# Pair sums and weight blocks placed by a scheduling pass, and operands made from PSUM, in an attention and two-expert kernel

## The chip, the cores and the metric

The kernel runs on one core of a Trainium2 chip. The metric is the device time of one execution in microseconds (us), the median of several runs. The profile shows one execution; its span runs from the first to the last instruction.

## The reference

Attention with pooled queries feeds two dense layers with their own activations. Batch 2, 8 heads, 1152 keys, head size 64; two neighbouring queries are averaged, so that 576 are left for each batch and 1152 tokens in all.

```python
q_pool = q.reshape(B, H, S // 2, 2, D).mean(axis=3)
scores = matmul(q_pool, k.T) / sqrt(D)
attn = exp(scores - max(scores)) / (sum(...) + 1e-9)
x = (attn @ v).transpose(0, 2, 1, 3).reshape(1152, 512)
h = x @ w_in1;  x = maximum(0.01 * h, h) @ w_out1       # 512 -> 2048 -> 512
h = x @ w_in2;  x = (h * tanh(softplus(h))) @ w_out2
```

The weights arrive as 64-bit floats.

## The kernel before

**Precision.** Each fp32 operand of a matmul is split into a rounded high part (a ScalarE cast) and a low part (source minus high part, by GpSimd or VectorE); each product is three matmuls, high by high, high by low and low by high.

**Attention.** Eight pairs of heads (four for each batch), nine tiles of 128 rows for each pair, 72 tiles `n`. A tile has scores (steps A, B, S on TensorE, three PSUM regions of 1152 columns), the maximum (M over 896 columns, N over 256, K for both, VectorE), the exponential (X, ScalarE, with row sums), nine transposes (T), and the split of the transposed tile (H on ScalarE, L on VectorE). P and Q take steps of the products with V and of the next pair's preparation. Scores of even tiles lie in PSUM columns 128 to 1280, those of odd ones in 1280 to 2432; a bank has 512 columns, so bank 2 holds the last 256 columns of even tiles and the first 256 of odd ones. Transposes and results use the columns from 2560.

**Pair sums.** The first layer multiplies 2x2 blocks by Strassen's method in Winograd's form (seven products in place of eight). Its right operands B11, T1, B22, T2, T3, B21 and T4 are blocks of the attention result and their differences. `pair_end_ops` scales a pair's result; `parts_of` then queues two steps (pairs 0 and 1 of a batch) or five (pairs 2 and 3), each a split and often a subtraction that the next step needs. Step V of the order takes one from the queue (`pop_part`). The sums of a pair overwrite those of the pair two before, and a buffer returns after four pairs. `last_recip` and `last_end` do the last pair after all tiles.

**Experts.** Two layers of eight slices of 256 hidden columns. `convert(i)` loads a slice's four blocks of 512 KB, turns each from 64-bit to 32-bit floats (two ScalarE activations, two VectorE bit operations, one GpSimd addition), makes the sums S1, S2, S4, S3 of the weights and splits all. `block_steps(i, g)` has the seven products of six matmuls for batch `g`, with the activation, split again by `finish`; `out_steps` multiplies by `w_out` and adds to `Y` in SBUF. `between(g)` makes layer 2's operands from `Y`.

**Order.** A `Recorder` takes every call as an operation with its memory cells and costs by a table. Up to tile 63 (CUT) all are issued as the hand-written PATTERN has them. The rest are list-scheduled: for each engine the earliest ready operation, ties by due time. An operation made by `lighter` may go to GpSimd or VectorE, whichever comes first; in the fixed order it is GpSimd. Each engine works through its own queue in that order. As all operations are replayed by the recorder, every row of the profile has line L391, and rows are told apart by tile: R holds split operands, F fp32 sums, I raw inputs and integers, PS is PSUM, `in_w_dram` the weights.

Of the kernel before, what the change touches and what calls it, by code (L numbers as in the profile page):

```python
# [19 lines left out]
SQ = S // 2  # L20
# [21 lines left out]
CUT = 63  # L42


class Op:
    __slots__ = ("alts", "reads", "writes", "preds", "succs", "due", "n", "unit", "eng", "end", "go")


class Recorder:
# [5 lines left out]
    def __init__(self, nc, file):  # L55
        self.nc, self.file, self.ops, self.open, self.cut = nc, file, [], None, None
        for name in self.ENGINES:
            setattr(self, name, Proxy(self, name))
# [12 lines left out]
    @contextmanager  # L71
    def either(self):

        assert self.open is None
        self.open = []
        yield
        made, self.open = self.open, None
        self.add([m[:4] for m in made], made[0][4], made[0][5])

    def add(self, alts, reads, writes):  # L80
        op = Op()
        op.alts, op.reads, op.writes, op.preds, op.succs = alts, reads, writes, set(), []
        op.n, op.eng, op.due = len(self.ops), None, 0.0
        self.ops.append(op)
# [22 lines left out]
    def cost(eng, method, outs, ins, kw):  # L107
# [29 lines left out]
    def cells(self, x):  # L137
# [10 lines left out]
        step = 512 if tag == "PS" else 32  # L148
# [15 lines left out]
    def plan(self):  # L164
# [22 lines left out]
        for op in reversed(self.ops):  # L187
            eng, _, occ, fin = op.alts[0]
            if eng != "PE":
                op.due += 3000  # L190
            for s in op.succs:
                lag = (occ if eng == "PE" and s.alts[0][0] == "PE" else fin + self.SYNC)
                op.due = min(op.due, s.due - lag)
# [15 lines left out]

        for op in self.ops[:self.cut]:  # L210
            place(op, op.alts[0])
        rest = self.ops[self.cut:]
        left = {op: sum(p.eng is None for p in op.preds) for op in rest}
        waiting = {op for op in rest if not left[op]}
        while waiting:
            best = {}
            for op in waiting:
                for alt in op.alts:
                    eng = alt[0]
                    t = max(free[eng], ready(op, eng))  # L220
                    key = (t if t > free[eng] + 5 else free[eng], op.due, op.n)
                    if eng not in best or key < best[eng][0]:
                        best[eng] = (key, op, alt)
            key, op, alt = min(best.values(), key=lambda b: b[0][0])
            place(op, alt)
# [7 lines left out]
        tail = sorted(order[self.cut:], key=lambda x: x[0].go)  # L233
        return order[:self.cut] + tail

    def emit(self):
        for op, calls in self.plan():
            for name, method, args, kw, line in calls:
                code = compile("\n" * (line - 1) + "method(*args, **kw)", self.file, "exec")
                exec(code, {"method": getattr(getattr(self.nc, name), method), "args": args, "kw": kw})  # L240
# [11 lines left out]
def tile_attention_moe_moe(  # L252
# [15 lines left out]
    F = sb.tile([128, 10832], F32, name="F")  # L268
# [3 lines left out]
    X = R[:, 0:XW].rearrange("p (g o s k t) -> p g o s k t", g=2, o=7, s=2, k=2)  # L272
    B11, B21, B22, T1, T2, T3, T4 = range(7)
# [26 lines left out]
    rlast = qsum  # L300
# [4 lines left out]
    ebuf = [F[:, 4832 + i * S:4832 + (i + 1) * S] for i in range(3)]  # L305
# [8 lines left out]
    traw = F[:, 4832:4832 + 2304].rearrange("p (o k t) -> p o k t", o=4, k=2)  # L314
    wraw = [I[:, 1024 * i:1024 * i + 1024] for i in range(2)]
    wa = [F[:, 8288 + 512 * i:8800 + 512 * i] for i in range(4)]
    wsum = I[:, 2048:2816].bitcast(F32).rearrange("p (o k f) -> p o k f", o=3, k=2)
    signs = PS[:, 3584:4096].bitcast(I32)
# [310 lines left out]
    def last_recip():  # L629
        after(("I", NPR - 1), mark=("R", 0))  # L630
        for first, c0, n in ((True, 0, 256), (False, 256, 320)):
            bank, col = t_take()
            for t in ((0, 1) if first else (2, 3)):
                c = col + 128 * (t % 2)
                nc.tensor.transpose(PS[:, c:c + 128], rwide[:, 128 * t:128 * t + 128], ident)
            if not first:
                nc.tensor.transpose(PS[:, col + 256:col + 384], rwide[:, 512:640], ident)
            nc.scalar.copy(out=rlast[:, c0:c0 + n], in_=PS[:, col:col + n])
            t_free.append(bank)

    def lighter(**kw):

        with rec.either():
            nc.gpsimd.tensor_tensor(**kw)
            nc.vector.tensor_tensor(**kw)

    def parts_of(p):
# [6 lines left out]
        def minus(to, a, b):  # L654
            lighter(out=to, in0=a, in1=b, op=ALU.subtract)

        def split(o, src):
            hi, lo = (X[:, g, o, i, k] for i in range(2))
            nc.scalar.copy(out=hi, in_=src)
            minus(lo, src, rounded(hi))  # L660

        if j < 2:
            return [
                [lambda: split(B11, q1), lambda: minus(q1, q2, q1)],
                [lambda: split(T1, q1)],
# [4 lines left out]
            [lambda: split(B22, q2), lambda: minus(t1, q2, t1)],  # L670
            [lambda: split(T2, t1), lambda: minus(b12, q2, b12)],
            [lambda: split(T3, b12)],
            [lambda: split(B21, q1), lambda: minus(q1, q1, t1)],
            [lambda: split(T4, q1)],
        ]

    def last_end():
        x = xu[(NPR - 1) % 4]
        after(("R", 0), *(("U", NPR - 1, u) for u in range(4)), *(("E", NPR - 2, i) for i in (True, False)))
        for h in (slice(TH, SQ), slice(0, TH)):  # L680
            lighter(out=x[:, h], in0=x[:, h], in1=rlast[:, h], op=ALU.mult)
            for step in parts_of(NPR - 1)[:3] if h.start else parts_of(NPR - 1)[3:]:
                for f in step:
                    f()
# [23 lines left out]
    banks = [0, 1, 2, 3, 4, 5, 6]  # L708

    def convert(i):  # L710
# [3 lines left out]
        l, s = divmod(i, NSL)  # L714
        w = (w1, w2)[l]
        wi, wo = WI[i % 2], WO[i % 3]

        def block(b):
            a = wa[b]
            ai = a.bitcast(I32)  # L720
            if not wide:
                nc.sync.dma_start(out=a, in_=w[s, b])
                return
            raw = wraw[(4 * i + b) % 2]
            v = raw.rearrange("p (n t) -> p n t", t=2)
            nc.sync.dma_start(out=raw, in_=w[s, b].bitcast(I32))
            nc.scalar.activation(out=a, in_=v[:, :, 1].bitcast(F32), func=AF.Copy, scale=2.0 ** -112)
            nc.scalar.activation(out=v[:, :, 0], in_=v[:, :, 0].bitcast(U32), func=AF.Copy, scale=2.0 ** -29)
            sign = v[:, :, 1] if i < 2 else signs
            nc.vector.tensor_scalar(out=sign, in0=v[:, :, 1], scalar1=-2 ** 31, scalar2=None, op0=ALU.bitwise_and)  # L730
            nc.vector.scalar_tensor_tensor(out=ai, in0=ai, scalar=3, in1=sign, op0=ALU.logical_shift_left,
# [337 lines left out]
```

## Time and profile before

| | |
|---|---|
| median of 3 runs | 705.27 us (704.4 to 707.95) |
| profiled execution: time, span | 707.48 us, 705.6 us |
| mean granted TensorE clock | 0.976 |
| busy: TensorE, its weight loads | 653.4 us (93%), 596.8 us |
| busy: VectorE, ScalarE, GpSimd | 539.3 us, 486.8 us, 459.0 us |
| TensorE waits for ScalarE's F, VectorE's R | 17.4 us (17 times), 14.9 us (17) |
| TensorE waits for ScalarE's R, VectorE's F | 7.4 us (8), 7.1 us (6) |

The attention ends near 300 us, the first layer near 510 us. PE is TensorE, DVE VectorE, ACT ScalarE, POOL GpSimd, SP SyncE.

### The profile page before, as it was taken

What the parts mean: (1) busy time and instruction counts of PE and PEld (TensorE: products, weight loads), DVE (VectorE), ACT (ScalarE), POOL (GpSimd) and SP (SyncE); (2) the same over time, 40 slices, a digit from 0 to 9 for tenths busy, and PEclk for the clock granted to TensorE, in tenths of its full rate; (3) what the DMA queues carried; (4) which work ended last, traced back from release to release, by engine and by line L of the source; (5) the groups of instructions that cost most, each with busy time, mean ns of one, the idle gap of its engine ahead of it and who ended that gap; (6) DMA issues with size and microseconds to landing.
All of it is one profiled execution on the core that took longest, in us unless ns stands there. A gap on an engine that the chain in (4) does not pass through costs nothing.

```text
span 705.6 us, 11839 instructions
## 1 busy us (share of the span) xinstructions
PE 653.4 (93%) x4154; PEld 596.8 (85%) x4154; DVE 539.3 (76%) x1033; ACT 486.8 (69%) x1039; POOL 459.0 (65%) x415
## 2 busy tenths in 40 slices
PE   7899999988979998739999999999899999999997
PEld 5799898977878987639989999999788888998896
DVE  4789897967768989997777778767988676775454
ACT  6789888877868888666766675757486666564330
POOL 6857577685766746986787665766787876574000
PEclk9999999998999999969999999999899999999999
DMA  4323232323212222313332223122112332310003
GB/s 130 117 77 113 82 94 92 80 75 77 80 42 80 47 68 79 116 61 99 110 121 90 91 91 120 60 78 102 31 61 91 119 100 81 121 60 0 1 1 134
DMA packets 18171, 57.77 MB, mean 82 GB/s; under 512 B 2368, under 2 KB 4928, under 8 KB 18112
## 3 DMA queue, kind: packets, MB, share of 16 engines
q1 hardware_dynamic: 16768, 52.18, 22.6%
q0 software_dynamic: 1120, 4.59, 2.8%
q8 instruction: 32, 0.52, 0.3%
q10 hardware_dynamic: 224, 0.26, 0.1%
q14 instruction: 27, 0.22, 0.1%
HBM read 47.71 MB, written 2.36 MB: 71 GB/s over the span
## 4 chain that ended last, share of the span: by engine, by line
PE 65%; POOL 9%; DVE 8%; ACT 6%; DMA 6%; issue 5%; SPq 0%; POOLq 0%; ACTq 0%; DVEq 0%
PE PS L391 65%; POOL R L391 4%; POOL F L391 4%; DVE R L391 4%; ACT F L391 3%; DVE F L391 3%; DMA I<-in_w_dram 3%; ACT R L391 3%; DMA F<-F 3%; DMA I<-in_kT_dram 1%; DVE I L391 0%; DVE PS L391 0%; POOL I L391 0%; ACT I L391 0%; ACT PS L391 0%
## 5 line engine op out<-in xcount | busy, mean ns | idle before, releaser
L391 PE MATMUL PS<-R 128*128 128x288 f32 (+4 forms) x3466 | 599.6, 328 | 42.0 <-ACT F L391 14.3
L391 PEld LDWEIGHTS PS<-R 128*128 128x128 f32 x3466 | 520.1, 192 | 86.6 <-ACT F L391 16.5
L391 DVE TENSOR_TENSOR R<-PS,R 128x384 fp32r<-128x384 f32 (+1 forms) x312 | 156.5, 520 | 54.9 <-ACT R L391 27.5
L391 POOL TENSOR_TENSOR R<-F,R 128x512 fp32r<-128x512 f32 (+4 forms) x116 | 141.3, 1233 | 56.3 <-ACT F L391 42.1
L391 DVE TENSOR_TENSOR F<-PS,F 128x512 f32<-128x512 f32 (+3 forms) x198 | 110.6, 562 | 58.8 <-PE PS L391 58.0
L391 POOL TENSOR_TENSOR F<-F,I 128x512 int32<-128x512 int32 x64 | 86.1, 1348 | 67.9 <-DVE F L391 29.3
L391 DVE TENSOR_REDUCE F<-PS 128x1 f32<-128x256 f32 (+1 forms) x144 | 106.7, 751 | 17.2 <-ACT F L391 9.2
L391 POOL TENSOR_TENSOR R<-I,R 128x576 fp32r<-128x576 f32 (+2 forms) x47 | 93.2, 1984 | 31.0 <-ACT R L391 19.4
L391 ACT CAST R<-PS 128x384 fp32r<-128x384 f32 x216 | 96.8, 485 | 21.7 <-PE PS L391 21.0
L391 PE MATMUL PS<-F 128*128 128x128 f32 x688 | 105.0, 280 | 6.6 <-ACT F L391 3.1
L391 POOL TENSOR_TENSOR F<-F 64x320 f32<-64x320 f32 (+6 forms) x80 | 67.3, 845 | 53.6 <-ACT R L391 24.3
L391 PEld LDWEIGHTS PS<-F 128*128 128x128 f32 x688 | 83.6, 143 | 18.3 <-DVE R L391 6.2
L391 ACT ACTIVATE F<-PS,F 128x1152 f32<-128x1152 f32 x72 | 88.5, 1230 | 3.5 <-PE PS L391 1.7
L391 ACT CAST R<-F 128x512 fp32r<-128x512 f32 (+5 forms) x114 | 62.7, 567 | 35.5 <-POOL F L391 20.5
L391 ACT ACTIVATE R<-PS 128x288 fp32r<-128x288 f32 x96 | 38.8, 407 | 59.3 <-DVE PS L391 55.9
L391 ACT COPY F<-PS 128x288 f32<-128x288 f32 (+2 forms) x130 | 50.7, 399 | 25.9 <-PE PS L391 20.6
L391 ACT ACTIVATE F<-I 128x512 f32<-128x512 f32 x64 | 43.3, 677 | 35.9 <-DMA I<-in_w_dram 28.9
L391 ACT CAST R<-I 128x576 fp32r<-128x576 f32 (+4 forms) x49 | 43.0, 877 | 8.2 <-PE PS L391 6.6
L391 DVE TENSOR_TENSOR R<-F,R 128x288 fp32r<-128x288 f32 (+2 forms) x44 | 41.4, 953 | 7.2 <-ACT F L391 6.1
L391 ACT ACTIVATE I<-I 128x512 int32<-128x512 uint32 x64 | 42.9, 675 | 0.0
L391 DVE TENSOR_SCALAR PS<-I 128x512 int32<-128x512 int32 x56 | 38.5, 687 | 1.5 <-DMA I<-in_w_dram 0.9
L391 ACT ACTIVATE PS<-PS 128x288 f32<-128x288 f32 x96 | 38.7, 404 | 0.0
(28 smaller groups left out, 250.9 us busy)
## 6 DMA issues: line engine op xcount, KB each, us to landing
I<-in_w_dram SPq DMA_DIRECT2D x64, 512.0 KB, 3.3
I<-in_vN_dram SPq DMA_DIRECT2D x8, 576.0 KB, 4.0
R<-R POOLq DMA_DIRECT2D x14, 320.0 KB, 4.2
I<-in_qT_dram SPq DMA_DIRECT2D x7, 576.0 KB, 4.6
I<-in_kT_dram SPq DMA_DIRECT2D x7, 576.0 KB, 4.1
out_dram<-F SPq DMA_DIRECT2D x8, 256.0 KB, 2.0
F<-F SPq DMA_DIRECT2D x16, 80.0 KB, 2.0
F<-F SPq DMA_DIRECT2D x16, 64.0 KB, 1.9
```

Source lines behind the costliest of these rows:

```text
L391: eng.dma_start(out=dst.bitcast(F32), in_=src)
```

## The change

Steps V of the attention and three weight blocks of slice 0 (`stage`, at tiles 12, 27 and 42) are recorded as loose. In the fixed part of the order the planner puts a loose operation ahead of the next one of its engine when, by its table, it would be ready for 300 ns and end no more than 150 ns after that one's start; an operation that needs one not yet placed forces it in. What is left at the cut joins the list schedule, which now has due times that count each engine's queue and may pick a more urgent operation that starts a little later. The last pair's operands and those between the layers are made by VectorE from values kept in PSUM. `lighter` is gone: subtractions are GpSimd's unless VectorE is named. The blocks around both changes of stage are issued in another order, with five PSUM banks instead of seven until the first slice is through, and the converted weight blocks have two buffers, `wa[i % 2]`. Operand X is laid out anew (half `k` outside), and the recorder tells PSUM apart by 128 columns instead of 512.

```diff
+SLIP = 150
+LOOK = 0.6
+STAGE = (12, 27, 42)
...
-            return (n + 62) / 0.96 * (1.4 if both else 1), (n + 145) / 0.96 * (1.4 if both else 1)
+            return (n + 62) / 0.96 * (3 if both else 1), (n + 145) / 0.96 * (3 if both else 1)
...
-        step = 512 if tag == "PS" else 32
+        step = 128 if tag == "PS" else 32
...
+        while heap:
+            op = heapq.heappop(heap)[2]
+            eng, _, occ, _ = op.alts[0]
+            op.due = min(op.due, back[eng] - occ)
+            if eng != "PE":
+                back[eng] = op.due
...
         for op in self.ops[:self.cut]:
+            if op.loose:
+                loose.append(op)
+                continue
+            for p in sorted(op.preds, key=lambda p: p.n):
+                if p.eng is None:
+                    force(p)
+            eng = op.alts[0][0]
+            start = max(free[eng], ready(op, eng))
+            found = True
+            while found:
+                found = False
+                for l in loose:
+                    if l.eng is None and l.alts[0][0] == eng and all(p.eng for p in l.preds):
+                        if max(free[eng], ready(l, eng) + 300) + l.alts[0][2] <= start + SLIP:
+                            place(l, l.alts[0])
+                            found = True
+                            break
             place(op, op.alts[0])
...
+                near = [x for x in ops if x[0] <= t0 + 5]
+                pick = min(near, key=lambda x: x[1:3])
+                soon = [x for x in ops if x[0] <= t0 + LOOK * pick[3].alts[0][2] and x[1] < pick[1] - 1000]
+                if soon:
+                    pick = min(soon, key=lambda x: x[1:3])
...
+    xraw = F[:, 9696:10720].bitcast(I32)
+    strips = bass.AP(tensor=PS.tensor, offset=PS.offset, ap=[list(PS.ap[0]), [2432, 2], [1, 128]]).bitcast(I32)
...
+    def last_pair():
+        low, high, third = (PS[:, c:c + TH] for c in (3072, 2592, 3584))
...
+        nc.vector.tensor_tensor(out=high, in0=high, in1=x[:, TH:SQ], op=ALU.mult)
+        minus(third, high, old[:, 0:TH], nc.vector)
+        part(T2, third)
+        part(B22, high)
+        minus(high, high, old[:, TH:SQ], nc.vector)
+        part(T3, high)
+        nc.vector.tensor_tensor(out=x[:, 0:TH], in0=low, in1=x[:, 0:TH], op=ALU.mult)
+        part(B21, x[:, 0:TH], nc.gpsimd)
+        minus(third, x[:, 0:TH], third, nc.vector)
+        part(T4, third)
...
-    banks = [0, 1, 2, 3, 4, 5, 6]
+    banks = [0, 1, 2, 3, 4]
+    def stage(i, b):
...
+        for c in range(2 if i < 2 else 1):
+            if i < 2:
+                to, top, sign = (y[:, 256 * c:256 * c + 256].rearrange("p (h n) -> p h n", h=2)
+                                 for y in (ai, v[:, :, 1], v[:, :, 1]))
+                sign = strips
+            else:
+                to, top, sign = ai, v[:, :, 1], signs
...
+        def final(d, half, keep):
...
+            y = Y[:, NTOK * d + t0:NTOK * d + t0 + TH]
+            nc.vector.tensor_tensor(out=ps if keep else y, in0=ps, in1=y, op=ALU.add)
...
+            def two():
+                ps = state["b11"][0]
+                state["b12"] = final(k, 1, False)
+                minus(ps, state["b12"], ps, nc.vector)
+                part(T1, ps, nc.vector)
...
-        for f in block_steps(0, 0):
-            f()
-        merged(block_steps(0, 1), out_steps(0, 0))
+        merged(block_steps(0, 0), [])
+        merged(out_steps(0, 0), [])
+        merged(block_steps(0, 1, late=True), [])
+        banks.extend((5, 6))
...
+            if i == NSL - 2:
+                merged(block_steps(i, 0) + block_steps(i + 1, 0), out_steps(i - 1, None))
+                merged(block_steps(i, 1), out_steps(i, 0))
+                convert(i + 2)
+                merged(between(0), block_steps(i + 1, 1))
+                merged(out_steps(i, 1), [])
+            elif i == NSL:
+                first = out_steps(i, None)
+                merged(between(1), block_steps(i, 0, late=True) + first[:4])
+                merged(block_steps(i + 1, 0, late=True), [])
+                merged(block_steps(i, 1, late=True), [])
+                convert(i + 2)
+                merged(block_steps(i + 1, 1, late=True), first[4:])
...
             if xq:
-                for f in xq.pop(0):
-                    f()
+                with rec.loose():
+                    for f in xq.pop(0):
+                        f()
...
+            if n in STAGE:
+                with rec.loose():
+                    stage(0, STAGE.index(n))
...
-        last_recip()
-        last_end()
+        last_pair()
```

## Rows read from the trace of the kernel before

**Rows 1.** The page: busy time of each engine, its share of the span, instructions.
```profile
PE 653.4 (93%) x4154; PEld 596.8 (85%) x4154; DVE 539.3 (76%) x1033; ACT 486.8 (69%) x1039; POOL 459.0 (65%) x415
```

**Rows 2.** By stretch: length, busy PE, PEld, DVE, ACT, POOL, clock, DMA share, GB/s.
```profile
280.00:320.00 40.00, 23.74 (x143) 21.07 (x143) 38.51 (x53) 26.29 (x61) 33.17 (x29) 0.83 0.25 83
285.00:300.00 15.00, 9.99 (x75) 9.02 (x74) 14.97 (x21) 10.62 (x26) 13.30 (x14) 1.00 0.28 89
...
500.00:512.00 12.00, 8.59 (x45) 8.12 (x44) 11.35 (x15) 4.31 (x9) 9.40 (x7) 0.72 0.14 44
516.00:548.00 32.00, 29.18 (x173) 25.52 (x172) 26.25 (x48) 24.17 (x57) 24.83 (x23) 1.00 0.26 83
400.00:490.00 90.00, 90.00 (x597) 86.33 (x596) 67.28 (x132) 57.15 (x131) 56.33 (x49) 1.00 0.28 94
```

**Rows 3.** The same columns, from one kT load to the next.
```profile
39.42:69.67 30.25, 30.08 (x217) 28.14 (x216) 27.72 (x60) 27.22 (x54) 20.54 (x18) 1.00 0.31 91
69.67:102.08 32.41, 31.07 (x220) 28.43 (x218) 28.14 (x61) 27.73 (x56) 22.87 (x21) 1.00 0.31 85
...
134.48:173.24 38.76, 33.52 (x220) 30.55 (x218) 28.87 (x61) 28.81 (x59) 26.72 (x26) 0.91 0.25 71
173.24:211.05 37.81, 32.50 (x220) 29.82 (x219) 28.65 (x61) 28.69 (x59) 26.73 (x26) 0.95 0.25 74
```

**Rows 4.** Timelines of ScalarE and TensorE: start, time, what, wait before it.
```profile
80.37 0.43 ACT L391 CAST R<-F 128x288 fp32r<-128x288 f32 x1 [1.74 <-POOL F L391]
...
159.42 0.43 ACT L391 CAST R<-F 128x288 fp32r<-128x288 f32 x1 [3.46 <-POOL F L391]
...
161.49 0.79 PE L391 MATMUL PS<-R 128*128 128x256 f32 x2 [3.97 <-ACT F L391]
```

**Rows 5.** Groups by shape, whole run: count, busy us, mean ns, waits before.
```profile
L391 POOL TENSOR_TENSOR F<-F,I 128x512 int32<-128x512 int32 x64 | 86.1, 1348 | 67.9 <-DVE F L391 29.3 <-ACT F L391 13.0 <-issue 10.8
...
L391 ACT ACTIVATE F<-I 128x512 f32<-128x512 f32 x64 | 43.3, 677 | 35.9 <-DMA I<-in_w_dram 28.9 <-POOL R L391 4.3 <-POOL I L391 2.6
...
L391 ACT CAST R<-F 128x288 fp32r<-128x288 f32 x28 | 11.8, 435 | 22.3 <-POOL F L391 17.3 <-DVE F L391 5.0
...
L391 DVE COPY F<-PS 128x256 f32<-128x256 f32 x8 | 3.4, 424 | 2.0 <-PE PS L391 2.0
```

**Rows 6.** A bank shared: an exponential in ScalarE's timeline, and VectorE's maxima as a group.
```profile
99.14 1.23 ACT L391 ACTIVATE F<-PS,F 128x1152 f32<-128x1152 f32 x1
...
L391 DVE TENSOR_REDUCE F<-PS 128x1 f32<-128x256 f32 x72 | 30.1, 420 | 15.0 <-ACT F L391 9.2 <-PE PS L391 3.4 <-ACT R L391 1.3
```

**Rows 7.** VectorE's groups by shape, 282 to 320 us.
```profile
L391 DVE TENSOR_TENSOR R<-F,R 128x288 fp32r<-128x288 f32 x9 | 11.7, 1331 | 0.0
L391 DVE TENSOR_TENSOR F<-F 128x288 f32<-128x288 f32 x7 | 9.3, 1341 | 0.2 <-ACT F L391 0.2
...
L391 DVE TENSOR_TENSOR PS<-PS,F 128x288 f32<-128x288 f32 x3 | 1.4, 451 | 0.0
```

**Rows 8.** Timelines of four engines, 290 to 316 us.
```profile
298.20 0.37 ACT L391 COPY F<-PS 128x256 f32<-128x256 f32 x1
...
300.64 1.89 POOL L391 TENSOR_TENSOR F<-F 64x256 f32<-64x256 f32 x2 [0.41 <-DMA F<-F]
...
309.27 6.43 DVE L391 TENSOR_TENSOR R<-F,R 128x288 fp32r<-128x288 f32 x4
...
291.86 2.59 PE L391 MATMUL PS<-R 128*128 128x288 f32 x19
...
311.41 2.82 PE L391 MATMUL PS<-R 128*128 128x288 f32 x10 [5.54 <-DVE R L391]
```

**Rows 9.** VectorE's group from 498 to 516 us, TensorE's wait, the table loads.
```profile
L391 DVE TENSOR_TENSOR R<-F,R 128x576 fp32r<-128x576 f32 x7 | 11.2, 1618 | 0.7 <-ACT R L391 0.7
...
505.45 1.65 PE L391 MATMUL PS<-R 128*128 128x256 f32 x6 [3.20 <-DVE F L391]
...
L391 ACT ACT_TABLE_LOAD x2 | 2.6, 1283 | 1.4 <-PEq L1057 1.4
```

More of the change, by code (lines that the diff above doesn't have):

```diff
@@ L42 @@
 CUT = 63
+SLIP = 150
+LOOK = 0.6
+STAGE = (12, 27, 42)
 class Op:
-    __slots__ = ("alts", "reads", "writes", "preds", "succs", "due", "n", "unit", "eng", "end", "go")
+    __slots__ = ("alts", "reads", "writes", "preds", "succs", "due", "n", "loose", "eng", "end", "go")
 class Recorder:
@@ L71, in either, with loose @@
     @contextmanager
[L72 to L75 removed]
+    def loose(self):
+        self.free = True
         yield
[L77 to L78 removed]
+        self.free = False
     def add(self, alts, reads, writes):
@@ L627, in invert_sums, with minus, split @@
                                 in1=one[0:64].unsqueeze(1).to_broadcast([64, 2, 64]), op=ALU.mult)
[L629 to L645, printed above, removed]
+    def minus(to, a, b, eng=None):
+        (eng or nc.gpsimd).tensor_tensor(out=to, in0=a, in1=b, op=ALU.subtract)
+    def split(pair, src, eng=None):
+        hi, lo = pair
+        nc.scalar.copy(out=hi, in_=src)
+        minus(lo, src, rounded(hi), eng)
     def parts_of(p):
@@ L652, in parts_of, with part @@
         q1, q2 = x[:, 0:TH], x[:, TH:SQ]
[L654 to L660, printed above, removed]
+        def part(o, src):
+            split([X[:, g, k, o, i] for i in range(2)], src)
         if j < 2:
             return [
-                [lambda: split(B11, q1), lambda: minus(q1, q2, q1)],
-                [lambda: split(T1, q1)],
+                [lambda: part(B11, q1), lambda: minus(q1, q2, q1)],
+                [lambda: part(T1, q1)],
             ]
@@ L755, in convert, with block_steps @@
         for f in range(2):
-            block(2 + f)
-            split([wo[:, h, f] for h in range(2)], wa[2 + f])
+            stage(i, 2 + f)
+            split([wo[:, h, f] for h in range(2)], a[2 + f])
     nblock = [0]
-    def block_steps(i, g):
+    def block_steps(i, g, late=False):
         l = i // NSL
@@ L795, in finish @@
             if name is None:
[L796 removed]
+                minus(gl, src, rounded(gh))
             else:
@@ new lines, in between @@
+        wo, gs = WO[i % 3], G[i % 2]
+        def final(d, half, keep):
+            t0 = SQ * g + TH * half
+            b = banks.pop(0)
+            ps = PS[:, 512 * b:512 * b + TH]
+            with rec.unit():
+                for f in range(2):
+                    for j, (ws, gi) in enumerate(PARTS):
+                        nc.tensor.matmul(out=ps, lhsT=wo[:, ws, f, 128 * d:128 * d + 128],
+                                         rhs=gs[f][:, gi, t0:t0 + TH], start=f == j == 0, stop=f == 1 and j == 2)
+            y = Y[:, NTOK * d + t0:NTOK * d + t0 + TH]
+            nc.vector.tensor_tensor(out=ps if keep else y, in0=ps, in1=y, op=ALU.add)
+            if keep:
+                return ps, b
+            banks.append(b)
+            return y
@@ new lines, in rows, with part, one_, three @@
+        def rows(k):
+            state = {}
+            def part(o, src, eng=None):
+                split([X[:, g, k, o, h] for h in range(2)], src, eng)
+            def one_():
+                state["b11"] = final(k, 0, True)
+                part(B11, state["b11"][0], nc.vector)
+            def two():
[3 more added lines that the diff above has]
+                part(T1, ps, nc.vector)
+            def three():
+                ps = state["b11"][0]
+                b22 = final(k + 2, 1, False)
+                minus(ps, b22, ps, nc.vector)
+                part(T2, ps, nc.vector)
+                part(B22, b22)
+                minus(state["b12"], b22, state["b12"])
+                part(T3, state["b12"])
+            def four():
+                ps, b = state["b11"]
+                b21 = final(k + 2, 0, False)
+                part(B21, b21)
+                minus(ps, b21, ps, nc.vector)
+                part(T4, ps, nc.vector)
+                banks.append(b)
+            return [one_, two, three, four]
@@ L909, in merged @@
+        return [f for two in zip(rows(0), rows(1)) for f in two]
     def merged(a, b):
```

198 lines of the change are left out of this document (97 added, 101 removed).

## Prediction

> **What bounds the kernel now.** I read the page first: its busy shares and the slices of the granted clock. TensorE is busy for 653.4 us [rows 1] of the span of 705.6, so what can be won lies in the 52 us in which it stands idle and in the stretches that follow, where it runs at the lower clock. Next I read the busy time by stretch, to see where those are. In the expert layers, away from their two ends, TensorE is busy for all of 90.00 us at clock 1.00 [rows 2]: nothing is to be had there, and nothing may be lost. The holes are in three places.
>
> The first is the attention. Cut at the starts of the kT loads, a pair of heads takes 30.25 us undisturbed, then 32.41, and two pairs take 38.76 and 37.81, though TensorE has 220 matmuls in each of the last three and is busy with them for 31.07 us in the plain one [rows 3]. ScalarE's timeline says why. A cast of a 128x288 pair sum stands in its queue until GpSimd has made that sum: 1.74 us at 80.37 us, the first of six such short waits (also near 113, 145, 184, 222 and 254), and 3.46 us at 159.42, the first of two long ones (the other is at 198.13). Behind the cast wait the casts and the exponential of the running tile, so VectorE and TensorE stop as well; TensorE comes back at 161.49 after 3.97 us [rows 4], and the clock of those pairs falls to a mean of 0.91 and 0.95 [rows 3]. These are the V steps of the hand-written order (pop_part).
>
> The second is the change from attention to experts: from 280 to 320 us TensorE is busy for 23.74 of 40, at clock 0.83, while VectorE is busy for 38.51 [rows 2]. The third is the change between the layers: 8.59 of 12 us from 500, at clock 0.72, and 29.18 of 32 from 516 [rows 2].
>
> **The change, part by part.** *Pair sums.* The pass takes each V step out of the fixed order and puts an instruction on its engine only where the planner sees room. Per disturbed pair the loss is its length less 31.07: 1.34 for one with a short wait, 7.7 and 6.7 for the two with a short and a long one [rows 3]. With the four short waits outside those two, 4 x 1.34 = 5.4, the attention has 19.8 us to give. Moved on GpSimd's queue, the sums pass the next pair's preparation, its two DMA issues and the additions of results; one put in too early holds these up by its own length. GpSimd has the time: it is busy for 26.7 us even in the long pairs, under the 31.07 that TensorE needs. ScalarE and VectorE have less room, 28.8 and 28.9 us of work there [rows 3]. The deadline stays (the sums of two pairs earlier are overwritten), and what has not been placed by then is forced in, waits and all. I take it that both long waits go, (7.7 - 1.34) + (6.7 - 1.34) = 11.7, and half of the six short ones, 4.0: gain 15.7, bounds 0 and 19.8.
>
> *Three weight blocks.* Each is one 512 KB load on SyncE's queue, two 128x512 activations of 0.677 us on ScalarE, four VectorE operations on 128x256 with their sign in two PSUM strips (nearest row: a 128x256 copy out of PSUM, 0.424), and one GpSimd addition of 1.348 [rows 5]. For three blocks that is 4.1, 12 x 0.424 = 5.1 and 4.0 us. The copies of attention results stand behind the loads on SyncE's queue, but a load waits only for its buffer, free since the block 15 tiles before. GpSimd and ScalarE hide their parts in idle time that the rows show; VectorE is the tightest. A second cost is that the strips lie in PSUM banks 0 and 4, which every tile's scores use. The rows show what sharing a bank does: the 128x256 maximum of a tile lies in bank 2 and needs TensorE's scores alone, yet these 72 maxima stood 9.2 us for ScalarE's F, 0.13 each; what writes F there is the exponential, 1.23 us long, which reads the neighbouring tile's columns of that bank [rows 6]. A strip operation can so cost from 0 to 0.424 + 1.23. I take half of VectorE's 5.1, since it is near its limit, and 12 x 0.13 = 1.5 of waits: 4.0; bounds 0 and 12 x 1.65 = 19.8.
>
> [...]
>
> *Attention to experts.* Idle there is 40 - 23.74 = 16.3; the lower clock is 40 x 0.17 = 6.8, of which the busy share, 23.74 / 40, counts: 4.0. So 20.3 us can be had [rows 2]. Today the last pair's products are SBUF work: VectorE's subtractions on 128x288 with both inputs in SBUF took 1.331 us (9) and 1.341 (7), while those with an input in PSUM took 0.451 [rows 7]. After the last attention result leaves PSUM at 298.20 come its copy, GpSimd's addition (from 300.64, 0.95 each of two) and then this work, whose last four take until 315.70; TensorE waits 5.54 us for it [rows 8]. In the new order nine operations of 0.45 are left, 4.1 us, with GpSimd's lone split and ScalarE's casts of 0.435 [rows 5] beside them: 301.6 + 4.1 = 305.7 at the latest, ten us sooner. Meanwhile the outputs of the first block (48 matmuls) and two products that don't need the last pair (12) now stand ahead: 60 x 0.136 (19 took 2.59 [rows 8]) = 8.2 us from 298, to 306. Three blocks less to convert also takes 3 x 1.35 us from GpSimd and VectorE's work on 128x512 from this stretch. What stays is VectorE's latency over the last tiles, 285 to 300, where TensorE idles for 15 - 9.99 = 5.0 us [rows 2], and I leave 1 more: gain 20.3 - 6.0 = 14.3, bounds 4 and 20.3. The two banks withheld at first cost nothing: a block holds three at once.
>
> *Between the layers.* Idle 3.4 and the clock 12 x 0.28 x 8.59/12 = 2.4, then 2.8 more idle: 8.6 to be had [rows 2]. Today VectorE makes the operands with seven 128x576 subtractions of 1.618 us, and TensorE waits 3.20 [rows 9]. The change makes each from PSUM in halves, at 0.451 [rows 7], while TensorE has other blocks' 42 products and 48 output matmuls, 12.2 us. I take all of the first stretch, 5.8, and half of the second: 7.2, bounds 0 and 8.6.
>
> *At nothing.* The subtraction of the slices' c22 moves to GpSimd for good, two a slice and each under the 1.348 us of a 128x512 operation [rows 5], so at most 2.7; GpSimd has 33.7 of 90 us free there [rows 2]. If that cover went, a slice would end up to 2.7 us later. The wider weight buffers and the planner's new due times I put at nothing because TensorE has no idle time to win in the slices, though they can lose some (below).
>
> Sum: 15.7 - 4.0 + 14.3 + 7.2 = 33.2. The profiled execution took 707.48, so 674.3; it lay 2.2 over the median of the runs shown, 705.27, so **672** by that median.
>
> **Rivals.**
> - *The pass finds no room.* VectorE and ScalarE are nearly full in the disturbed pairs, and waits forced at the deadline are the old ones; the blocks still cost 4.0. For it: ScalarE's and VectorE's busy time. Against: GpSimd, whose lateness makes the waits, has 4 us free. Gain 14.3 + 7.2 - 4.0 = 17.5: 688.
> - *The strips serialise the tiles.* The full 19.8 is paid: 15.7 - 19.8 + 21.5 = 17.4, the same 688, with new VectorE waits for ScalarE instead of the old ScalarE waits for GpSimd. For it the bank wait of [rows 6], against it its mean of 0.13.
> - *All comes.* 19.8 + 20.3 + 8.6 = 48.7 with the blocks hidden: 657.
> - *Only the attention gains*, since the last tiles' latency and GpSimd's conversions set the changes' length: gain 11.7, 694.
> - *The new planner loses in the slices* (the other side). Its look-ahead lets an engine idle for up to 0.6 of an operation for a more urgent one, and its due times now count each engine's queue. In 14 plain slices of some 23.5 us (156 matmuls each; 597 took 90 us [rows 2]) TensorE has no slack at all. It decides once a slice loses 33.2 / 14 = 2.4 us; at 3 us, 42 lost, 714. A layer-2 activation drawn ahead of layer 1's last ones adds table loads of 1.283 [rows 9]. Against it: operands there are ready well before TensorE needs them.
>
> **How the numbers follow.** My forecast has 0.53 (its own range 662 to 683), all 0.10, no room 0.11, strips 0.08, attention alone 0.06, the planner's loss 0.08, and 0.04 that gains and losses cancel. The range 657 to 694 leaves out the last two, 0.12, and a little at each edge. A median of this kernel can be told from no change at about 0.5%, 3.5 us. Faster 0.88, same 0.04, slower 0.08.
>
> **What would show it.** Right: pairs of 31 to 33 us throughout, and no cast of 128x288 on ScalarE waiting 3 us for GpSimd; the three weight loads near 60, 110 and 165 us; no VectorE operation of 1.3 us from 285 to 320, TensorE over 33 of those 40 us and its clock at 1.00; no clock dip between layers. Wrong: pairs still of 37 us (pass), VectorE's strip operations waiting a microsecond for ScalarE (strips), or TensorE under 89 of 90 us in the slices (planner).

## The result, and the profile after

The changed kernel takes **673.68 us** (median of 4 runs, 673.58 to 675.88) beside 705.34 (704.40 to 707.95): a ratio of 0.9553 [0.9521, 0.9585], 31.7 us less. The forecast was 672.0. The profiled execution took 675.88 us.

The page: TensorE is busy for 9 us less than in [rows 1], and stands idle for 30 us where it was 52.

```profile
span 674.1 us, 11885 instructions
PE 644.1 (96%) x4179; PEld 589.6 (87%) x4179; DVE 504.6 (75%) x1040; ACT 490.1 (73%) x1051; POOL 467.7 (69%) x450
```

Busy time by stretch, with the columns of [rows 2]. The first five rows run from one kT load to the next and answer to [rows 3]; 280 to 320 and 500 to 512 are the times of [rows 2]. The fifth pair now ends 14 us earlier than before, so by its place in the program the stretch from 280 to 320 is now 266 to 306, the row behind it.

```profile
38.68:68.92 30.24, 30.09 (x217) 28.12 (x216) 27.73 (x60) 27.75 (x55) 20.50 (x18) 1.00 0.35 109
68.92:102.72 33.80, 31.57 (x220) 28.21 (x218) 29.43 (x65) 28.24 (x56) 23.10 (x21) 1.00 0.29 81
102.72:133.00 30.28, 30.28 (x220) 28.48 (x219) 28.00 (x61) 28.35 (x57) 23.07 (x22) 1.00 0.36 109
133.00:166.79 33.79, 31.97 (x224) 28.46 (x222) 30.11 (x66) 29.85 (x60) 26.62 (x26) 1.00 0.29 82
166.79:197.09 30.30, 30.15 (x217) 27.98 (x216) 27.45 (x59) 28.46 (x60) 26.45 (x25) 1.00 0.36 109
...
280.00:320.00 40.00, 37.83 (x274) 35.92 (x273) 26.46 (x61) 29.24 (x72) 35.74 (x38) 1.00 0.18 58
266.04:306.04 40.00, 34.97 (x224) 31.06 (x222) 26.52 (x63) 27.91 (x66) 31.54 (x35) 0.91 0.18 59
...
500.00:512.00 12.00, 12.00 (x76) 11.05 (x75) 8.42 (x16) 9.68 (x23) 7.74 (x6) 1.00 0.12 39
```

Three things are to be seen. First, the pairs of 38.76 and 37.81 us are gone, and TensorE's clock is 1.00 in all five. Second, two pairs are not plain: 33.80 and 33.79, some 3.5 us over their neighbours. These hold VectorE's work on the first two weight blocks, which were loaded one pair earlier. SyncE's timeline:

```profile
52.23 0.42 SPq L786 DMA_DIRECT2D F<-in_w_dram  x1
...
109.17 0.58 SPq L786 DMA_DIRECT2D F<-in_w_dram  x1
...
171.59 0.33 SPq L786 DMA_DIRECT2D F<-in_w_dram  x1
```

Third, both changes of stage are fuller: by place, 34.97 us busy of 40 at 0.91 for the first (23.74 at 0.83 before), and for the second no hole is left near 500 us (8.59 of 12 at 0.72 before). A smaller hole stands earlier, in the last tiles of the attention, 240 to 280 us, where TensorE is busy for 31.4 of 40 and its clock falls to 0.66 in the last quarter:

```profile
240.00:280.00 40.00, 31.43 (x191) 26.38 (x190) 29.38 (x66) 29.43 (x58) 18.60 (x21) 0.91 0.17 56
270.00:280.00 10.00, 9.19 (x45) 7.78 (x46) 7.29 (x18) 7.39 (x17) 6.79 (x9) 0.66 0.18 53
```

What makes the pairs with a block longer? Lines of the code are told apart in this trace: L560 is the scores, L591 the exponential, L796 and L797 are the two VectorE operations that take a weight's sign into the strips and bring it back. Timelines of the pair with the first block (start, time, engine, what, wait before it):

```profile
82.19 0.42 DVE L797 SCALAR_TENSOR_TENSOR F<-F,PS 128x256 int32<-128x256 int32 x1 [0.89 <-PE PS L560]
...
89.24 0.42 DVE L797 SCALAR_TENSOR_TENSOR F<-F,PS 128x256 int32<-128x256 int32 x1 [1.87 <-ACT F L591]
...
82.66 0.73 PE L560 MATMUL PS<-R 128*128 128x512 f32 x2 [0.52 <-DVE F L797]
...
85.59 1.44 PE L560 MATMUL PS<-R 128*128 128x256 f32 x8 [0.98 <-DVE PS L796]
...
82.70 1.23 ACT L591 ACTIVATE F<-PS,F 128x1152 f32<-128x1152 f32 x1 [0.59 <-DVE F L797]
```

The strips are columns 0 to 127 and 2432 to 2559, the scores 128 to 2431: no number passes between them. Yet in these rows VectorE waits for the scores (0.89 us) and for the exponential (1.87), the scores (0.52 and 0.98) and the exponential (0.59) for VectorE. What they have in common are banks 0 and 4, by the kernel's count of 512 columns to a bank. In TensorE's list of waits from 60 to 235 us (total, times, longest) these two lines are the only ones of over half a microsecond:

```profile
PE PS L560 <- DVE F L797: 2.8, 5, 0.8
PE PS L560 <- DVE PS L796: 2.0, 3, 1.0
```

### The profile page after: what moved, and what is told of

Read it like the earlier page. It is cut to its first block, busy times and chain, and to the rows that moved or that the text cites. A ratio compares the mean times of both kernels' runs of the same rounds, so it can differ in the third digit from the quotient of the medians.

```text
span 674.1 us, 11885 instructions
## 1 busy us (share of the span) xinstructions
PE 644.1 (96%) x4179; PEld 589.6 (87%) x4179; DVE 504.6 (75%) x1040; ACT 490.1 (73%) x1051; POOL 467.7 (69%) x450
## 4 chain that ended last, share of the span: by engine, by line
PE 43%; POOL 6%; DMA 4%; ACT 3%; DVE 3%; issue 2%; DVEq 0%; POOLq 0%; ACTq 0%
PE PS L843 19%; PE PS L928 10%; PE PS L918 10%; DMA I<-in_w_dram 4%; POOL R L684 2%; POOL F L799 2%; PE PS L958 2%; PE PS L615 1%; PE PS L650 1%; ACT R L856 1%; ACT F L787 1%; DVE PS L796 1%; ACT PS L857 1%; DVE F L910 0%; DVE F L797 0%
## 5 line engine op out<-in xcount | busy, mean ns | idle before, releaser
L843 PE MATMUL PS<-R 128*128 128x288 f32 x1344 | 206.0, 297 | 3.5 <-DVE F L851 1.5
L684 POOL TENSOR_TENSOR R<-F,R 128x512 fp32r<-128x512 f32 (+1 forms) x124 | 126.3, 1031 | 73.7 <-ACT F L857 54.0
L560 PE MATMUL PS<-R 128*128 128x512 f32 (+2 forms) x480 | 111.5, 361 | 16.6 <-ACT F L591 7.7
L633 DVE TENSOR_TENSOR R<-PS,R 128x384 fp32r<-128x384 f32 x216 | 112.3, 549 | 9.6 <-ACT R L628 9.1
L910 DVE TENSOR_TENSOR F<-PS,F 128x512 f32<-128x512 f32 (+2 forms) x140 | 83.6, 600 | 40.9 <-PE PS L928 23.3
L928 PE MATMUL PS<-R 128*128 128x512 f32 x432 | 108.5, 390 | 0.0
L628 ACT CAST R<-PS 128x384 fp32r<-128x384 f32 x216 | 95.6, 485 | 17.6 <-PE PS L615 14.4
L918 PE MATMUL PS<-R 128*128 128x320 f32 (+2 forms) x552 | 101.3, 322 | 0.4 <-DVE R L861 0.3
L560 PEld LDWEIGHTS PS<-R 128*128 128x128 f32 x480 | 75.2, 193 | 29.4 <-ACT F L591 8.3
L591 ACT ACTIVATE F<-PS,F 128x1152 f32<-128x1152 f32 x72 | 88.4, 1228 | 11.9 <-PE PS L560 4.2
L650 PE MATMUL PS<-R 128*128 128x256 f32 (+1 forms) x576 | 94.8, 304 | 0.0
L928 PEld LDWEIGHTS PS<-R 128*128 128x128 f32 x432 | 77.8, 188 | 12.4
L861 DVE TENSOR_TENSOR R<-PS,R 128x288 fp32r<-128x288 f32 x96 | 43.6, 455 | 52.5 <-ACT PS L857 51.8
L569 DVE TENSOR_REDUCE F<-PS 128x1 f32<-128x896 f32 x72 | 78.0, 1083 | 1.2 <-PE PS L560 1.1
```

Of the source, the lines that this page charges most:

```text
L560: nc.tensor.matmul(out=PS[:, pc:pc + w], lhsT=lq, rhs=KS[p % 2][:, h, kc:kc + w], start=(i == 0), stop=(i == len(ops) - 1))
L591: nc.scalar.activation(out=ebuf[n % 3], in_=PS[:, a:e], func=AF.Exp, scale=SCALE, bias=mx[:, n % 3, 2:3], accum_out=rcol(n))
L628: nc.scalar.copy(out=pt_dst(n, g, 0), in_=t_src[n, g][1])
L633: nc.vector.tensor_tensor(out=pt_dst(n, g, 1), in0=src, in1=rounded(pt_dst(n, g, 0)), op=ALU.subtract)
L650: nc.tensor.matmul(out=PS[:, bank[1]:bank[1] + n], lhsT=vs[:, k, 128 * h:128 * h + 128], rhs=PT[:, slot, s, k, 0:n], start=(k == 0 and s = ...
L684: (eng or nc.gpsimd).tensor_tensor(out=to, in0=a, in1=b, op=ALU.subtract)
```

## The experiments

One table for all: median, ratio with its interval, and from one profiled execution, whose time stands there too, "five pairs" (from the kT load near 38 us to the fifth one after it) and "rest" (from there to the end of the span). That execution lay 2.2 us over the median in the changed kernel, so its rest may be as much too long. The ratios compare each kernel with the kernel before as it ran beside it, at 703.89 to 705.34 us. In the kernels named "SBUF", the signs of slices 0 and 1 stay in SBUF.

| kernel | us | ratio to before | profiled | five pairs | rest |
|---|---|---|---|---|---|
| before | 705.34 | | 707.48 | 171.63 | 494.6 |
| changed | 673.68 | 0.9553 [0.9521, 0.9585] | 675.88 | 158.41 | 477.0 |
| 1: SBUF | 664.96 | 0.9421 [0.9392, 0.9450] | 664.56 | 156.85 | 467.9 |
| 2: no block early | 676.61 | 0.9588 [0.9568, 0.9607] | 676.52 | 152.14 | 485.6 |
| 3: sums in fixed order | 689.70 | 0.9780 [0.9760, 0.9800] | 690.28 | 174.30 | 477.2 |
| 4: no look-ahead | 681.80 | 0.9669 [0.9648, 0.9690] | 680.81 | 158.69 | 482.2 |
| 5: last pair from SBUF | 680.29 | 0.9656 [0.9631, 0.9681] | 682.90 | 158.73 | 483.3 |
| 6: between from SBUF | 681.53 | 0.9670 [0.9652, 0.9688] | 681.49 | 158.61 | 484.3 |
| 7: before, with the pass | 677.77 | 0.9613 [0.9593, 0.9634] | 678.88 | 152.18 | 485.7 |
| 8: SBUF, block at tile 30 | 663.10 | 0.9410 [0.9383, 0.9438] | 662.84 | 155.26 | 467.8 |
| 9: SBUF, no block early | 665.67 | 0.9448 [0.9419, 0.9477] | 664.11 | 152.15 | 473.2 |
| 10: SBUF, price kept | 659.20 | 0.9359 [0.9325, 0.9393] | 657.88 | 152.15 | 466.9 |
| 11: SBUF, cells of 512 | 665.66 | 0.9448 [0.9418, 0.9478] | 665.59 | 155.73 | 470.4 |
| 12: 10, no block early | 663.47 | 0.9425 [0.9397, 0.9453] | 663.29 | 152.18 | 472.1 |

**1. Signs in SBUF.** The theory: the strips' banks cost the 3.5 us a block. The rival: VectorE has no room for the blocks' operations, wherever the sign lies. The first edit only leaves the planner's price of this operation as it was.

```diff
-            both = method in ("tensor_tensor", "scalar_tensor_tensor") and all(
+            both = method == "tensor_tensor" and all(
...
-                sign = strips
+                sign = top
```

> The strips alone are undone: the signs of slices 0 and 1 stay in SBUF, in place, and the planner's price for that operation is left as it was. Theory (bank waits): the two pairs with a staged block go from 33.8 us back to about 31, as do the third's, since what costs 3.5 us a block is waiting for scores and exponentials in banks 0 and 4; the hole between 240 and 290 us shrinks too; 660 to 667 us in all. Rival (work): VectorE and ScalarE are full and the block's own operations cost the 3.5 us wherever the sign lies: 672 to 676. Rival (ports): with both inputs in SBUF the operations lengthen beside GpSimd, from 0.42 us to 0.8 or more: 674 to 680.

The theory holds for the total: 664.96, 8.7 us less, and TensorE's list of waits from 100 to 235 us has no line for L796 or L797 any more. The pairs with the first two blocks:

```profile
68.32:98.92 30.60, 30.60 (x220) 28.11 (x219) 28.88 (x65) 28.10 (x56) 21.73 (x19) 1.00 0.32 91
...
129.13:164.60 35.47, 33.11 (x224) 29.70 (x223) 32.14 (x66) 29.75 (x60) 26.98 (x26) 0.95 0.27 78
```

The first is plain at 30.60, though VectorE has the same 65 instructions in it. The second is longer than with strips. Its timelines, and the group of the operation by shape (shortest, median, longest in ns):

```profile
143.94 2.63 POOL L394 TENSOR_TENSOR R<-I,R 64x1152 fp32r<-64x1152 f32 x1
...
144.27 2.58 DVE L797 SCALAR_TENSOR_TENSOR F<-F 128x256 int32<-128x256 int32 x1
...
147.38 0.55 PE L615 MATMUL PS<-F 128*128 128x128 f32 x3 [2.24 <-DVE R L633]
...
L797 DVE SCALAR_TENSOR_TENSOR F<-F x6: 412/416/2580, 80.4 to 210.0; 128x256 int32<-128x256 int32 x6
L797 DVE SCALAR_TENSOR_TENSOR F<-F,I x8: 407/760/1479, 250.7 to 290.4; 128x256 int32<-128x256 int32 x8
```

With both inputs in SBUF, one operation of 0.416 us took 2.58: it began while GpSimd's subtraction ran and ended 0.28 us after it. Of the eight later ones in the last line, half took 0.76 us or more, up to 1.48. So of the two ways the strips cost more, but SBUF has a price too. And the gain over the changed kernel lies mostly not in the pairs (1.6) but in the rest (9.1; by the medians some 7). The groups of both lines in the changed kernel, 30 to 300 us, say why:

```profile
L797 DVE SCALAR_TENSOR_TENSOR F<-F,PS x14: 410/420/423, 82.2 to 283.8; 128x256 int32<-128x256 int32 x14
L797 DVE SCALAR_TENSOR_TENSOR I<-I,PS x2: 408/410/411, 261.5 to 264.1; 128x256 int32<-128x256 int32 x2
...
L796 DVE TENSOR_SCALAR PS<-I x10: 418/428/429, 245.2 to 282.0; 128x256 int32<-128x256 int32 x10
L796 DVE TENSOR_SCALAR PS<-F x6: 419/428/428, 74.8 to 211.1; 128x256 int32<-128x256 int32 x6
```

All 32 operations of slices 0 and 1 go by the strips, not only the 12 of the three early blocks; the other 20 meet the last tiles' scores, in the hole from 240 to 280 us (from 235 to 300 VectorE waits 3.3 us for the scores before these lines).

**2. No block early**, strips kept: `STAGE = ()`.

> No weight block is placed in the attention; all of slice 0 is converted after tile 63, still with the strips. Bank waits: pairs of 30.3 us throughout, 10 us sooner at tile 63, but three blocks more of 3.5 us or more in the crowded stretch after it: 671 to 682. If the blocks hurt only in the attention: 663 to 667. If they were worth placing there (VectorE and GpSimd full after tile 63): above 682.

676.61. The five pairs fall to 152.14, so the early blocks cost 6.3 there; the rest grows by 8.6 (10.8, if the changed kernel's is 2.2 too long), as these blocks now meet the last tiles too: kernel 9 differs from this one in the signs alone, and its rest is 12.4 shorter. What the early place wins net is 2.9 us, and the two intervals overlap.

**3. Pair sums in the fixed order**, all else as changed.

```diff
-                with rec.loose():
-                    for f in xq.pop(0):
-                        f()
+                for f in xq.pop(0):
+                    f()
```

> The pair sums go back to their fixed places in the order (not loose); all else as changed. Theory: the short and long waits of ScalarE's casts for GpSimd come back, six of 1.7 and two of 3.5 us with the clock's fall after the long ones: 20 to 25 us more, 693 to 699. Rival: the gain of the attention comes from the order of other things, and the sums' places matter little: below 680.

689.70: 16.0 more, beside 15.7 in the forecast, and under the 20 to 25 expected here. The pairs, and ScalarE's waits for GpSimd's pair sums from 20 to 285 us (total, times, longest), here and in the kernel before:

```profile
67.27:100.18 32.91, 30.90 (x220) 28.45 (x219) 29.74 (x65) 28.84 (x57) 24.14 (x22) 1.00 0.31 84
...
132.59:171.74 39.15, 33.32 (x226) 30.50 (x225) 31.12 (x66) 30.50 (x61) 27.98 (x27) 0.96 0.25 72
...
ACT R L688 <- POOL F L684: 15.9, 8, 3.7
```

```profile
ACT R L391 <- POOL F L391: 17.8, 9, 3.5
```

The old waits are back; in the changed kernel the list has no such line. The blocks add only 0.5 and 0.4 us to 32.41 and 38.76 [rows 3]: TensorE stands idle there anyway. The expectation put the old waits on top of the changed kernel's time, in which each of these two blocks costs 3.5 us. What a part costs depends on the holes that the others leave.

**4. No look-ahead**: `LOOK = 0.0`. The planner then never lets an engine wait for a more urgent operation.

> The look-ahead of the list schedule is off (0 in place of 0.6 of an operation); due times as changed. If the look-ahead costs TensorE time in the slices (the rival on the other side): faster than 672, and TensorE's idle time of 2.6 us in the slices goes. If it is worth something in the crowded change from attention to experts: 677 to 690. If it does nothing: 672 to 676.

681.80, so the look-ahead is worth 8.1 us; from 320 to 520 us TensorE idles for 5.2 us more. Here, and under it the changed kernel:

```profile
320.00:470.00 150.00, 145.48 (x975) 139.05 (x974) 105.75 (x217) 100.05 (x233) 110.37 (x103) 1.00 0.31 102
470.00:520.00 50.00, 48.26 (x323) 45.48 (x322) 39.34 (x88) 38.35 (x92) 42.68 (x43) 1.00 0.26 85
```

```profile
320.00:470.00 150.00, 149.30 (x1008) 143.66 (x1007) 110.11 (x224) 104.62 (x239) 113.45 (x107) 1.00 0.30 99
470.00:520.00 50.00, 49.62 (x329) 46.73 (x328) 38.43 (x80) 36.79 (x85) 38.09 (x37) 1.00 0.23 70
```

**5. The last pair's operands from SBUF.** ScalarE copies the reciprocals out of PSUM, and the same products, subtractions and splits work on SBUF; block order and planner stay.

```diff
+        r = qsum
+        nc.scalar.copy(out=r[:, TH:SQ], in_=high)
+        nc.scalar.copy(out=r[:, 0:TH], in_=low)
...
-        minus(third, high, old[:, 0:TH], nc.vector)
-        part(T2, third)
+        minus(t1, q2, t1, nc.vector)
+        part(T2, t1)
```

> The last pair's operands are made in SBUF again: ScalarE copies the transposed sums out of PSUM, and VectorE's products and subtractions have both inputs in SBUF (B21's low part on GpSimd, as now). Theory of the prediction (SBUF subtractions of 1.3 us are the chain that TensorE waits for): the last operand some 8 to 10 us later, TensorE idle after 285 us again: 680 to 684. Rival: now that the outputs of slice 0 stand ahead of the second batch's products, the chain is covered: 673 to 676.

680.29, 6.6 more, within what was expected; the stretch from 270 to 310 us here, and in the changed kernel:

```profile
270.00:310.00 40.00, 31.06 (x190) 27.43 (x191) 25.46 (x54) 23.95 (x54) 27.82 (x28) 0.89 0.18 59
```

```profile
270.00:310.00 40.00, 37.02 (x241) 33.70 (x242) 27.25 (x63) 27.85 (x68) 33.59 (x37) 0.91 0.18 57
```

**6. The operands between the layers from SBUF**, in 128x576 and in the old order of blocks; planner and buffers stay.

```diff
+        minus(t1, b12, b11, nc.vector)
+        part(T1, t1, nc.vector)
+        part(B21, b21, nc.gpsimd)
+        minus(t2, b22, t1, nc.vector)
...
-            if i in (NSL - 1, NSL + 1):
```

> The operands between the layers are made from the sums in SBUF as before the change, in 128x576 operations shared by VectorE and GpSimd, and the blocks of slices 6 to 9 stand in the old order. Theory: the hole of 9 us around the layers' border comes back, 680 to 684. Rival: the planner's look-ahead and due times fill it, 673 to 677.

681.53, 7.9 more, as expected. The stretch from 480 to 500 us here, and in the changed kernel:

```profile
480.00:500.00 20.00, 13.67 (x75) 12.81 (x74) 13.90 (x21) 10.62 (x23) 13.31 (x10) 0.80 0.00 1
```

```profile
480.00:500.00 20.00, 19.62 (x131) 18.40 (x130) 15.45 (x35) 15.88 (x40) 14.84 (x18) 1.00 0.29 88
```

**7. The pass alone**: the kernel before, with step V recorded as loose and the placing of loose operations; old planner, signs, buffers and changes of stage.

```diff
+            while found:
+                found = False
+                for l in loose:
...
+                with rec.loose():
+                    for f in xq.pop(0):
+                        f()
```

> The kernel before with one part of the change alone: pair sums loose and put into place by the pass; no staged blocks, old list schedule, old changes of stage. Theory: pairs of 30.3 us throughout, so 18 to 20 us less: 685 to 688. If the pass needs the new planner or the attention's gain is used up by the old change to the experts: 690 to 700.

677.77, 27.1 less than the 704.86 of the kernel before beside it: most of the 31.7 us, and far more than expected. All other parts together add some 4. The five pairs, the stretch behind them, and ScalarE's waits as in experiment 3:

```profile
38.92:191.10 152.18, 151.79 (x1089) 141.43 (x1088) 139.93 (x300) 139.86 (x279) 117.98 (x110) 1.00 0.31 91
191.10:290.00 98.90, 85.74 (x580) 78.61 (x578) 91.05 (x176) 82.95 (x176) 72.19 (x70) 0.94 0.25 81
...
ACT R L424 <- POOL F L424: 0.5, 1, 0.5
```

The pairs are plain, TensorE idle for 0.4 us in 152: 19.5 won. Another 8.9 come from the rest (7.6 by the medians). The second row answers to this one of the kernel before, from the end of its five pairs through the change to the experts:

```profile
211.05:320.00 108.95, 88.73 (x587) 78.89 (x586) 99.18 (x181) 85.10 (x179) 74.09 (x69) 0.94 0.23 73
```

As many matmuls, but for seven, take ten us less, and TensorE idles for 13.2 in place of 20.2. The trace shows where. For 90 us behind the five pairs the two kernels are level (557 matmuls before, 562 here); they part in the next 20 us, the change itself. First the kernel before, then kernel 7, with VectorE's 128x288 operations that have both inputs in SBUF, from 262 to 300 us:

```profile
301.05:321.05 20.00, 9.04 (x40) 8.19 (x39) 19.29 (x23) 11.09 (x26) 14.71 (x11) 0.66 0.15 52
```

```profile
281.10:301.10 20.00, 16.25 (x101) 16.25 (x102) 15.48 (x30) 10.88 (x25) 15.90 (x15) 0.76 0.24 80
...
L424 DVE TENSOR_TENSOR R<-F,R 128x288 fp32r<-128x288 f32 x10 | 7.5, 762 | 0.0
L424 DVE TENSOR_TENSOR F<-F 128x288 f32<-128x288 f32 x4 | 7.1, 1805 | 0.0
```

These operations take VectorE 14.6 us (14 of them); in the kernel before they took 21.0 (16) in the same place [rows 7]. So the pass also shortens the last pair's chain on VectorE. What there makes them shorter was not tried.

**8 to 12. Can the blocks be had for nothing?** All have their signs in SBUF. Kernel 8 moves the second block from tile 27 to 30 (`STAGE = (12, 30, 42)`), to part it from GpSimd's subtraction.

> Signs in SBUF as in the run with 664.96 us, and the second block recorded at tile 30 in place of 27. There one operation of VectorE with both inputs in SBUF took 2.58 us beside a GpSimd subtraction of 2.66, and its pair 35.5 us in place of 30.3. Theory (the two share a way into SBUF, and it is chance which operation meets a long one): at another place this pair goes back to 30.3 to 31 and the time falls to 660 to 662. Rival: that pair is long for another reason: 664 to 666.

663.10, which leaves it open: VectorE's operation landed beside the same subtraction again (2.57 us at 144.17), the pair took 33.90. Kernel 9 is kernel 1 with `STAGE = ()`; kernel 10 is kernel 1 with the planner's old price.

```diff
-            both = method == "tensor_tensor" and all(
+            both = method in ("tensor_tensor", "scalar_tensor_tensor") and all(
```

> The signs of slices 0 and 1 lie in SBUF and no block is placed during the attention. If placing blocks early pays once the four operations of a block no longer meet the scores' PSUM banks, this is slower than the kernel with signs in SBUF and three placed blocks (664.96 us): 669 to 674, with the idle time of TensorE between 240 and 290 us as in the kernel that places none. If the early blocks only pay for themselves, it is 662 to 667. Both agree that the five pairs of heads after the first take 151 to 153 us.

> The signs lie in SBUF, and the planner keeps its threefold price for a VectorE operation with both inputs in SBUF, so that the second operation of a block is placed elsewhere. If the 35.47 us of one pair of heads come from that operation lying beside GpSimd's 2.63 us addition, then no pair takes over 31.5 us unless another such operation takes over 1.5 us, and the time is 660 to 664 as long as the blocks still find their places. If the pair's length has another cause (the load of the block, ScalarE's casts), one pair still takes over 33 us, and the time stays at 664 to 667.

Kernel 9 takes 665.67, as kernel 1 does: the early blocks cost 4.7 in the pairs and win 5.3 in the rest. Kernel 10 takes **659.20**, 14.5 under the changed kernel and the best of all. At three times the price the second VectorE operation of a block finds no room among the tiles. Only the first block is then loaded, cast and has its signs taken out early; its other half waits until 229 us, and so does the buffer that the next block needs. Windows by kT load, and the operation by shape:

```profile
67.26:97.52 30.26, 30.26 (x220) 28.30 (x219) 28.29 (x63) 28.11 (x56) 21.68 (x20) 1.00 0.33 91
...
127.76:158.49 30.73, 30.66 (x220) 28.24 (x219) 28.12 (x61) 28.73 (x59) 25.91 (x25) 1.00 0.31 90
...
L797 DVE SCALAR_TENSOR_TENSOR F<-F x6: 418/422/1032, 229.5 to 246.5; 128x256 int32<-128x256 int32 x6
```

No pair is over 30.73, as the theory of GpSimd's subtraction expected; the time is a little under its range. But this does not part the theory from its rival, the load and casts of the block: the second block is not loaded among the tiles at all. That the long operation made the long pair rests on the two traces in which it met the subtraction, and on TensorE's wait of 2.24 us behind it; what makes the rest of the 5.2 us by which that pair was over a plain one stays open. Kernel 11 is kernel 1 with PSUM in cells of 512 columns, kernel 12 is kernel 10 with `STAGE = ()`.

> The signs lie in SBUF, and the planner knows PSUM in cells of a whole bank of 512 words again, as the kernel before had it. If the finer cells let operations on two parts of one bank be ordered freely and the chip pays for that with waits, the time is no longer than 664.96 us: 660 to 665. If the finer cells are worth something, the planner puts work later that could run: 667 to 675, with the loss in the slices after 320 us.

> The signs lie in SBUF, no block is placed during the attention, and the planner keeps its threefold price for a VectorE operation with both inputs in SBUF. Against the kernel that places no block at the low price (665.67 us) only the price differs, against the one that places blocks at the high price (659.2 us) only the placing. If the 6.5 us between those two come from the block that was cast early, this takes 664 to 667. If they come from the price, by which later operations of the first slices are ordered otherwise, it takes 658 to 661.

Kernel 11 is at 665.66, between the two ranges: the finer cells are worth nothing that can be measured. Kernel 12, at 663.47, is between its two as well: against kernel 10 the half block that is made early is worth 4.3 us, and the price by itself 2.2 (665.67 to 663.47), the intervals of which overlap.

## Why the prediction was right

The sum was right within 2 us, but by luck: the gain of the pair sums was put 11.4 us too low, and two other terms were 12.4 us too favourable together. The mechanisms of the pair sums, of the strips and between the layers were right.

**Pair sums: mechanism right, size too small.** Forecast 15.7, at most 19.8; the pass alone gave 27.1. The step that failed is "its length less 31.07". The pair with 31.07, called plain there, has a short wait itself, and TensorE's busy time in a disturbed pair is not what it needs: the same 220 matmuls now take 30.28 us. Of the loss in the five pairs, which the forecast put at 17.1 and of which it took 11.7 and four half short waits, 14.4 in all, 19.5 came back. The pass found room for all, though VectorE and ScalarE were as full as [rows 3] say: the first rival is out. The gain in the rest, 7.6 to 8.9 us, was not seen: the prediction allowed 1.3 for two half waits there and credited the change to the experts to other edits.

**Weight blocks: mis-sized, and in the wrong place.** Forecast -4.0, of it 1.5 for 12 bank waits; the strips alone cost 8.7 (kernel 1). The step that failed is the count of twelve: the diff moves the signs of all eight blocks of slices 0 and 1 from SBUF to the strips, 32 operations, and the removed line `sign = v[:, :, 1] if i < 2 else signs` showed it. By 32 operations the cost is 0.27 us each, twice the 0.13 of [rows 6] and far from the bound of 1.65; it is a quotient, and single waits were up to 1.87 us. The rival "strips serialise" so names the right mechanism at less than half its price. VectorE's own work, put at half of 5.1, costs little where it is not held: kernel 1's pair with the first block is 0.35 us over the plain one.

In the trace eight waits of the scores are for operations that share no column with them, 4.8 us from 60 to 235. That the bank is what ties them is read from the layout alone: no run has the strips in another bank.

**Attention to experts: right in place, too large for its cause.** Forecast 14.3. The marks are there by the clock time that was named: TensorE busy for 37.83 of 40 us at 1.00, and VectorE's subtractions at 0.45 us (four of 128x288 with an input in PSUM, mean 450 ns). By place it is 34.97 at 0.91. And taking the operands back to SBUF costs 6.6 (kernel 5). The step that failed is to credit all of the idle time there to the operands and the order of blocks: the pass alone takes seven us of it (kernel 7), and the hole that remains, 240 to 280 us, leaves TensorE idle for 8.6, more than the 6.0 left over in the forecast. Nor was the 1.33 us a fixed price of two inputs in SBUF: in kernel 7 the operations of that shape took 0.762 us in the same place (ten, with R) and 1.805 (four, F alone).

**Between the layers: right.** Forecast 7.2, measured 7.9 (kernel 6, which takes back the order of blocks with the operands), and no clock dip: 1.00 from 470 to 530 us.

**At nothing: right as a sum, not for its reason.** The slices lost little: 0.7 us idle from 320 to 470, and 1.0 in the kernel before, 14 us later. But the reason given, that the slices have no idle time to win, hides what the look-ahead does: without it the changed kernel loses 8.1 us (kernel 4), with 5.2 more of idle time from 320 to 520, most of it in the slices, where [rows 2] show no slack. So the rival "the new planner loses" has part of its mechanism, at a fifth of its 42 us, and the look-ahead, which that rival blamed, prevents it. Whether the due times or another edit open these holes was not tried: no kernel here has the old planner with the other changes.

The measured terms add up to 27.1 - 8.7 + 6.6 + 7.9 = 32.9, beside 31.7 measured, but that proves nothing. They come from different kernels, leave out the look-ahead's 8.1, and are not additive, as kernel 3 shows: the pass is worth 27.1 alone and 16.0 as the last of the parts.

## What to carry to other kernels

A scratch area in an idle corner of a busy PSUM bank was not free here: its operations waited for the scores and exponentials of that bank, up to 1.87 us, and held them up, at 0.27 us for each of 32 (8.7 in all). So count all the instructions that a diff moves there, not only those that come to mind first. The undisturbed stretch, not the busy time of a disturbed one, is the floor to measure a loss against. And a part's worth should be taken both alone and as the last one: a weight block placed early cost 0.5 us while other waits left holes, and 3.5 once these were closed.

## What the runs showed of the hardware

VectorE's operation on 128x256 with both inputs in SBUF, 0.416 us (the median of six in kernel 1), took 2.58 beside GpSimd's subtraction of 2.63 that had begun 0.33 us before, and 2.57 in kernel 8, where the two met again with the same 0.33 between their starts. It ended 0.28 and 0.27 us after the subtraction. What the two contend for, no run shows. The surprise is in the sum: with the signs in SBUF one of six such operations was held among the tiles, and eight later ones took up to 1.48 us, median 0.76; even so this was 8.7 us cheaper than the bank that was chosen in its place.
